# Segment means in two whole operations, and the layer norm of the last two w2 tiles moved into the first w3 groups

## The chip, the cores and the metric

The kernel runs on one core of a Trainium2 chip. The metric is the device time of one execution in microseconds (us). A core has five engines that run at the same time, each with its own queue of instructions: TensorE (PE in the profile, with its weight loads as PEld), VectorE (DVE), ScalarE (ACT), GpSimd (POOL) and SyncE (SP), which issues most of the DMA transfers. They wait for each other by semaphores. Work that lies beside a busy TensorE costs nothing; what makes TensorE wait is added to the time.

## The reference

Two blocks follow each other on x of 2048 tokens by 1024 columns: attention over 64 segments of 32 tokens with an 8-token memory carried from segment to segment, and an MLP with four shifts of the columns. Cut to what matters:

```
h = layernorm(x) * (1 + ca) + sa
x = x + ga * A(h, mem0, Wq, Wk, Wv, Wo)      # 32 heads of 128
h = layernorm(x) * (1 + cb) + sb
x = x + gb * B(h, w1, w2, w3, w4)

def B(x):
    h  = gelu(layernorm(x) @ w1)             # 1024 x 1024
    x1 = x + shifts(h) @ w2                  # 1024 x 1024
    return x1 + gelu(layernorm(x1) @ w3) @ w4   # 1024 x 3584, 3584 x 1024
```

`sa, ca, ga, sb, cb, gb` come from `silu(c) @ w_mod`. Weights and x are bf16.

## The kernel before

Tokens lie in 16 tiles of 128; a transposed operand has the 1024 columns on 128 partitions in 8 pieces (KT = 8). The stages run in this order: the first layer norm, which writes `hh` (h transposed); a first set of projections ("wave 0") for two pairs of heads; a first guess of the segment memories; then attention, in which the projections of later heads and the scores and outputs of earlier heads are woven together; the projection with Wo; the second layer norm; w1; w2; and the stage with w3 and w4. Two orders are at work. Up to w2 a scheduler orders each engine's instructions, within what program order, `keep_order` and added dependencies ask. The stage with w3 and w4 stands under `manual_schedule`, so there the order of the program is the order on each engine.

**Segment means.** The guess of the memories starts from the mean of h over each segment. While the layer norm runs, PE sums the columns of each segment into the PSUM tile `hsum` (L427). `g_prep` (L456) turns the sums into `hbar`, a 128x8x64 tile in bf16: each of the 8 pieces is scaled by its column of `cm` and shifted by its column of `sm_`, the even ones on ScalarE (L462), the odd ones on VectorE (L460); then the first segment, which has another shift, is written over with `m0` in place of `sm_` (L464, L465). `g_v` (L477) multiplies `hbar` with Wv, in eight groups, each with a 1 MB chunk of weights (`wchunk`) and a PSUM tile from a ring of three; `g_o` (L491) does the same with Wo. Between these groups the rest of wave 0 is placed, one projection (L318) at a time. Its PSUM tiles come from the same ring and are emptied by `evac` (L122 on ScalarE, L127 on VectorE).

**Sums of h.** The projections of later heads use a scheme with seven products instead of eight for a 2x2 block, which needs sums and differences of quarters of `hh`: S1, S2, S4 and A21 for each of two halves of the tokens, eight VectorE operations on 128x1920 elements (L519 to L522). In the kernel before they stand behind `ph.close()`, in program order, each held by `keep_order`. The last of the four writes over a quarter of `hh`, so it has to wait until wave 0 has read it. The weights have their own sums (`T_units`, L566 to L569), which wait for the load of the weights. The products are at L623, their joins on VectorE at L595. Scores are at L717, exp at L721, the mask at L723, outputs at L734, and the scaling of the outputs, which frees their PSUM tile, at L741.

**w2 and its layer norm.** `Ba(t)` multiplies tile t with w2 (L1170) into two PSUM tiles; VectorE adds u (`u2`) into `x1b`, a 128x1024 tile in f32, and sums the rows as it goes (L1172). `x1b` is stored in DRAM (L1173). `ln_sums` makes the normalized tile `z` from it: the negative mean `ln_nm` on VectorE (L1147, L1148); the sum of squares on ScalarE (L1150); three operations of one column on GpSimd (`ln_ve` L1152, `ln_rstd` L1154, `ln_nmr` L1156); and the scaling on ScalarE (L1157). `Bb(t)`, one tile later, transposes `z` by DMA into `z2a` (tiles 0 to 7) or `z2b` (tiles 8 to 15). The tiles of this stage, `u2`, `x1b` and `z`, come from the pool `x2_t` with four buffers each. The pools of the next stage lie in part where those of `x2_t` lay, and a first write into such a tile waits for the last reader of what lay there.

**w3.** The stage takes the tokens in two pairs of 512, tiles 0 to 7 and then 8 to 15, each in seven groups over w3 (`w3_stage`) and then w4 (`w4_stage`). A group is again seven products, each for two blocks q of 128 columns and four matmuls long (L1244). They go into the PSUM tiles `bank_b`, `bank_e` and `bank_d`. After the first product into `bank_b`, ScalarE takes a copy (`snap`, L1209), and the third product, which adds to `bank_b`, waits for that copy; between them lies one product into `bank_e`. VectorE joins banks with copies (`join`, L1252) and ScalarE applies gelu (L1248). At the end of a group stand the sums of the next group's weights on VectorE (`w3_sums`, L1098) and one-seventh of the addend units, in which SP loads `x1b` and `x1` back and GpSimd makes the final addend (L1218 to L1223). The sums of `z2a` and the first weights' sums are woven into the last w2 tiles (from tile 10 on). `z2b` is used from the end of pair 0 on.

Of the kernel before, what the change touches and what calls it, by code (L numbers as in the profile page):

```python
# [9 lines left out]
BF16 = mybir.dt.bfloat16  # L10
F32 = mybir.dt.float32
F16 = mybir.dt.float16
I32 = mybir.dt.int32
ACT = mybir.ActivationFunctionType
ALU = mybir.AluOpType
# [4 lines left out]
P = 128  # L20
S = 2048
D = 1024
KT = D // P
# [37 lines left out]
def kernel(ctx, tc, A_x, A_mem0, A_Wq, A_Wk, A_Wv, A_Wo, A_seg_len, B_x, B_w1, B_w2, B_w3, B_w4, c, w_mod, out,  # L61
# [105 lines left out]
    def first_pass(late_hook):  # L167
# [287 lines left out]

        def g_prep():  # L456
            gs["hbar"] = sb1.tile([P, KT, NSEG], BF16, name="hbar")
            for kt in range(KT):
                if kt % 2:
                    nc.vector.tensor_scalar(gs["hbar"][:, kt, :], hsum[:, kt, :], cm[:, kt:kt + 1], sm_[:, kt:kt + 1], ALU.mult, ALU.add)  # L460
                else:
                    nc.scalar.activation(gs["hbar"][:, kt, :], hsum[:, kt, :], ACT.Identity, bias=sm_[:, kt:kt + 1], scale=cm[:, kt:kt + 1])  # L462
            first = sb1.tile([P, KT], F32, name="first")
            nc.vector.tensor_tensor(first[:], hsum[:, :, 0], cm[:], ALU.mult)  # L464
            nc.vector.tensor_tensor(gs["hbar"][:, :, 0], first[:], m0[:], ALU.add)  # L465
            gs["vbarT"] = sb1.tile([P, H, NSEG], BF16, name="vbarT")

        def g_v(g):
# [42 lines left out]
        def f16(ap):  # L511
            return ap.bitcast(F16)

        hA = []
        for p in range(2):
            c0, c1 = slice(2 * p * CH, (2 * p + 1) * CH), slice((2 * p + 1) * CH, (2 * p + 2) * CH)
            A11, A12, A21, A22 = hh[:, 0:4, c0], hh[:, 4:8, c0], hh[:, 0:4, c1], hh[:, 4:8, c1]
            S1, S2, S4 = (hsp.tile([P, 4, CH], F16, name=f"hs{j}{p}")[:] for j in (1, 2, 4))
            keep_order(nc.vector.tensor_tensor(S1, A21, A22, ALU.add))  # L519
            keep_order(nc.vector.tensor_tensor(S2, S1, A11, ALU.subtract))  # L520
            keep_order(nc.vector.tensor_tensor(S4, A12, S2, ALU.subtract))
            keep_order(nc.vector.tensor_tensor(f16(A21), A11, A21, ALU.subtract))  # L522
            hA.append((A11, A12, S4, A22, S1, S2, f16(A21)))
        LA = ExitStack()
        vp = LA.enter_context(tc.tile_pool(name="up_v", bufs=1))
# [604 lines left out]
        def z_sums(pair):  # L1130
# [6 lines left out]
            return [lambda: dve(S1, A21, A22, ALU.add), lambda: dve(S2, S1, A11, ALU.subtract),  # L1137
                    lambda: dve(S3, A11, A21, ALU.subtract), lambda: dve(S4, A12, S2, ALU.subtract)]

        LT2 = ExitStack()  # L1140
        tp = LT2.enter_context(tc.tile_pool(name="x2_t", bufs=4))
        bsm = LT2.enter_context(tc.tile_pool(name="x2_sm", bufs=8))

        def ln_sums(smp, dst, src, sums):

            nm = smp.tile([P, 1], F32, name="ln_nm")
            nc.vector.tensor_tensor(nm[:], sums[:, 0:1], sums[:, 1:2], ALU.add)  # L1147
            nc.vector.tensor_scalar(nm[:], nm[:], -1.0 / D, None, ALU.mult)  # L1148
            sq = smp.tile([P, 1], F32, name="ln_sq")
            nc.scalar.activation(dst, src, ACT.Square, bias=nm[:], accum_out=sq[:])  # L1150
            ve = smp.tile([P, 1], F32, name="ln_ve")
            nc.gpsimd.tensor_scalar(ve[:], sq[:], 1.0 / D, EPS, ALU.mult, ALU.add)  # L1152
            rstd = smp.tile([P, 1], F32, name="ln_rstd")
            nc.gpsimd.tensor_tensor(rstd[:], ve[:], mhalf[:], ALU.pow)  # L1154
            nmr = smp.tile([P, 1], F32, name="ln_nmr")
            nc.gpsimd.tensor_tensor(nmr[:], nm[:], rstd[:], ALU.mult)  # L1156
            nc.scalar.activation(dst, src, ACT.Identity, bias=nmr[:], scale=rstd[:])  # L1157

        def Ba(t):
            def f():  # L1160
                ts = slice(t * P, (t + 1) * P)
                u = tp.tile([P, D], BF16, name="u2")
                nc.sync.dma_start(u[:], u_d[ts, :])
                x1b = tp.tile([P, D], F32, name="x1b")
                sums = bsm.tile([P, 2], F32, name="ln_sums")
                for n2 in range(2):
                    acc = acc_tile()
                    for kt in range(KT):
                        o = 2 + t * P + SHIFT[kt]
                        nc.tensor.matmul(acc[:], lhsT=h1T[:, kt, o:o + P], rhs=w2s[:, kt, n2 * 512:(n2 + 1) * 512], start=(kt == 0), stop=(kt == KT - 1))  # L1170
                    cs = slice(n2 * 512, (n2 + 1) * 512)
                    nc.vector.scalar_tensor_tensor(x1b[:, cs], acc[:], 1.0, u[:, cs], ALU.mult, ALU.add, accum_out=sums[:, n2:n2 + 1])  # L1172
                nc.scalar.dma_start(x1b_d[ts, :], x1b[:])  # L1173
                z = tp.tile([P, D], BF16, name="z")
                ln_sums(bsm, z[:], x1b[:], sums)
                zs[t] = z
            return f

        def Bb(t):
            return lambda: nc.sync.dma_start_transpose(z2s[t // 8][:, :, t % 8 * P:(t % 8 + 1) * P], zs[t][:])  # L1180

        for i, u in enumerate(lagged(Ba, Bb, list(range(NTT)), lag=1)):
            u()
            if i in (4, 8):
                load_upto(ring_ctr[0])
            if i == 10:
                zu = z_sums(0) + w3_sums(0)
            if i >= 10:
                for f in zu[2 * (i - 10):2 * (i - 9)]:
                    keep_order(f())  # L1190
# [36 lines left out]
        def w3_stage(pair):  # L1227

            hq = [[hq_p.tile([P, 14, 512], BF16, name=f"hq{a}{f}") for f in range(2)] for a in range(2)]
            A11, A12, S4, A22, S1, S2, S3 = zsum[pair]
            add = addend_units(pair)
            for g in range(7):
                n = pair * 11 + g
                load_upto(n + 2)
                B11, B21, B22, T4, T1, T2, T3 = ready[n]
                st = [{} for _ in range(2)]

                def prod(bank, A, B, start):  # L1240
                    for q in range(2):
                        acc = st[q][bank]
                        for k in range(4):
                            nc.tensor.matmul(acc[:], lhsT=B[:, k, q * P:(q + 1) * P], rhs=A[:, k, :], start=(start and k == 0), stop=(k == 3), skip_group_check=True)  # L1244
                        yield q

                def gelu(a, f, q, src):
                    nc.scalar.activation(hq[a][f][:, g * 2 + q, :], src[:], ACT.Gelu_apprx_tanh)  # L1248

                def join(a, f, q, bank, s):  # L1250
                    t = stm.tile([P, 512], F32, name="join")
                    nc.vector.tensor_tensor(t[:], st[q][bank][:], st[q][s][:], ALU.add)  # L1252
                    gelu(a, f, q, t)

                for q in range(2):
                    st[q]["b"] = psb.tile([P, 512], F32, name="bank_b")
                for q in prod("b", A11, B11, True):
                    st[q]["s1"] = snap(stA, st[q]["b"])
                for q in range(2):
                    st[q]["e"] = pse.tile([P, 512], F32, name="bank_e")  # L1260
                for q in prod("e", A12, B21, True):
                    join(0, 0, q, "e", "s1")
                dve(T4, B21, T2, ALU.subtract)
                for q in prod("b", S2, T2, False):
                    st[q]["s2"] = snap(st2, st[q]["b"])
                for q in range(2):
                    st[q]["d"] = psd.tile([P, 512], F32, name="bank_d")
                for q in prod("d", S1, T1, True):
                    st[q]["s5"] = snap(stA, st[q]["d"])
                for q in prod("b", S3, T3, False):  # L1270
                    join(1, 1, q, "b", "s5")
                for q in prod("d", S4, B22, False):
                    join(0, 1, q, "d", "s2")
                for q in prod("b", A22, T4, False):
                    gelu(1, 0, q, st[q]["b"])
                for u in w3_sums(n + 1) if g < 6 else []:
                    u()
                for u in add[16 * g // 7:16 * (g + 1) // 7]:
                    u()
            return hq  # L1280
# [97 lines left out]
        with tc.manual_schedule():  # L1378
            for pair in range(2):
                hq = w3_stage(pair)  # L1380
                if pair == 0:
                    LZA.close()
                    rsp = LZ2.enter_context(tc.tile_pool(name="x3_rs", bufs=8))
                    outp = LZ2.enter_context(tc.tile_pool(name="x3_o", bufs=4))
                w4_stage(pair, hq, rsp, outp, late_hook if pair == 1 else None)
# [700 lines left out]
```

## Time and profile before

Three runs took 1485.69, 1487.77 and 1492.43 us; the median is 1487.77. The profiled execution:

| engine | busy us | share of the span | instructions |
|---|---|---|---|
| PE | 1423.4 | 96% | 9198 |
| PEld | 754.6 | 51% | 9254 |
| DVE | 895.3 | 60% | 1946 |
| ACT | 685.7 | 46% | 1443 |
| POOL | 371.8 | 25% | 526 |

The busy share of PE in 40 slices of 37 us is 9 tenths or more in all but the first slice and two others. The places of the change on the profile's clock: the segment means at 63 to 73 us, the sums of h at 112 to 123 us, the border between w2 and w3 at 1128 to 1150 us. A row of the timeline gives start, duration, engine, line and work (output, input, shapes); in brackets stands how long the engine had been idle and who released it. Releasers are inferred from the semaphores, and where an engine waited for several, the last one is named.

### The profile page before, as it was taken

What the parts mean: (1) busy time and instruction counts of PE and PEld (TensorE: products, weight loads), DVE (VectorE), ACT (ScalarE), POOL (GpSimd) and SP (SyncE); (2) the same over time, 40 slices, a digit from 0 to 9 for tenths busy, and PEclk for the clock granted to TensorE, in tenths of its full rate; (3) what the DMA queues carried; (4) which work ended last, traced back from release to release, by engine and by line L of the source; (5) the groups of instructions that cost most, each with busy time, mean ns of one, the idle gap of its engine ahead of it and who ended that gap; (6) DMA issues with size and microseconds to landing.
All of it is one profiled execution on the core that took longest, in us unless ns stands there. A gap on an engine that the chain in (4) does not pass through costs nothing. (4 is left out here: it accounts for less than half of the span.)

```text
span 1488.6 us, 24703 instructions
## 1 busy us (share of the span) xinstructions
PE 1423.4 (96%) x9198; PEld 754.6 (51%) x9254; DVE 895.3 (60%) x1946; ACT 685.7 (46%) x1443; POOL 371.8 (25%) x526
## 2 busy tenths in 40 slices
PE   5898999999999999999998999999998999999998
PEld 3465555565555555555554444444443444444443
DVE  5318777777676777667653244354245668776684
ACT  2715666665665665655552021123465661046400
POOL 7402100000000000000001223213023665646525
PEclk9999999999999999999999999999999999999999
DMA  9677968867777877778579999994398774477812
GB/s 306 204 284 150 192 156 186 193 152 168 167 171 178 191 155 181 156 169 179 109 172 303 352 312 363 327 236 149 97 310 232 230 252 160 135 236 248 278 39 78
DMA packets 404149, 303.48 MB, mean 204 GB/s; under 512 B 199082, under 2 KB 356778, under 8 KB 402226
## 3 DMA queue, kind: packets, MB, share of 16 engines
q1 hardware_dynamic: 365904, 242.06, 61.5%
q10 hardware_dynamic: 29330, 30.89, 6.8%
q0 software_dynamic: 8784, 28.85, 6.6%
q8 instruction: 74, 1.21, 0.4%
q14 instruction: 57, 0.47, 0.1%
HBM read 200.56 MB, written 50.63 MB: 169 GB/s over the span
## 5 line engine op out<-in xcount | busy, mean ns | idle before, releaser
L905 PE MATMUL acc<-wstream,OTc 128*128 128x512 bf16 x940 | 207.8, 379 | 7.7 <-DMA OTc<-OTx_d 3.3
L623 PEld LDWEIGHTS <-T 128*128 128x128 f16 x1408 | 131.4, 98 | 120.4 <-issue 4.4
L591 ACT COPY snap<-acc 128x480 f32<-128x480 f32 x264 | 146.1, 564 | 91.5 <-PE acc L623 83.5
L623 PE MATMUL acc<-hh,T 128*128 128x480 bf16 (+1 forms) x704 | 163.9, 367 | 0.0
L623 PE MATMUL acc<-hs,T 128*128 128x480 f16 x704 | 159.6, 369 | 0.7 <-ACT snap L591 0.6
L905 PEld LDWEIGHTS <-OTc 128*128 128x128 bf16 x960 | 93.3, 98 | 118.8 <-issue 3.9
L759 POOL DMA_DIRECT2D OTx_d<-OT x32 | 24.8, 775 | 439.2 <-DMA OT<-O 372.9
L1244 PEld LDWEIGHTS <-ring 128*128 128x128 f16 (+1 forms) x784 | 77.7, 99 | 106.6 <-issue 16.5
L721 ACT ACTIVATE E<-ps_s 99x495 bf16<-99x495 f32 (+2 forms) x160 | 87.3, 546 | 45.8 <-PE ps_s L717 45.2
L623 PE MATMUL acc<-hh,wq 128*128 128x480 bf16 x464 | 103.9, 366 | 0.0
L741 DVE TENSOR_TENSOR O<-ps_o,rin_all 99x384 bf16<-99x384 f32 (+1 forms) x192 | 97.1, 509 | 3.7
L1098 DVE TENSOR_TENSOR ring<-ring 128x1024 f16<-128x1024 bf16 (+1 forms) x64 | 86.5, 1370 | 5.6 <-PE bank_b L1295 5.2
L734 PE MATMUL ps_o<-V,E 99*128 99x129 bf16 (+1 forms) x704 | 79.6, 220 | 10.6 <-DMA V<-VT 4.8
L595 DVE TENSOR_TENSOR KT<-acc,snap 128x480 bf16<-128x480 f32 x116 | 74.9, 654 | 22.3 <-PE acc L623 19.9
L1295 PEld LDWEIGHTS <-hq 128*128 128x128 bf16 (+1 forms) x560 | 54.7, 98 | 66.1
L1209 ACT COPY snap<-bank_b 128x512 f32<-128x512 f32 x72 | 40.5, 582 | 100.1 <-PE bank_b L1295 58.3
L734 PEld LDWEIGHTS <-E 99*128 99x128 bf16 (+1 forms) x704 | 56.3, 98 | 48.5 <-issue 8.0
L1013 ACT ACTIVATE u<-x,ln_nmr,ln_rstd 128x1024 bf16<-128x1024 f32 x16 | 19.7, 1232 | 127.4 <-DVE ln_nmr L1012 101.6
L723 DVE TENSOR_TENSOR E<-E,maskB 99x495 bf16<-99x495 bf16 (+1 forms) x128 | 48.0, 376 | 49.3 <-ACT E L721 47.4
L1295 PE MATMUL bank_b<-ring,hq 128*128 128x512 f16 (+1 forms) x334 | 73.1, 379 | 0.1
L595 DVE TENSOR_TENSOR VT<-acc,snap 128x480 bf16<-128x480 f32 x90 | 58.0, 650 | 24.9 <-PE acc L623 20.9
L1248 ACT ACTIVATE hq<-join 128x512 bf16<-128x512 f32 x84 | 52.8, 630 | 41.7 <-DVE join L1252 41.7
(243 smaller groups left out, 2527.8 us busy)
## 6 DMA issues: line engine op xcount, KB each, us to landing
wstream<-in_A_Wo_dram SPq DMA_DIRECT2D x31, 1024.0 KB, 11.5
OTx_d<-OT POOLq DMA_DIRECT2D x32, 512.0 KB, 7.0
wstream<-in_B_w_dram SPq DMA_DIRECT2D x28, 512.0 KB, 5.7
OTc<-OTx_d SPq DMA_DIRECT2D x14, 1024.0 KB, 9.5
ring<-in_B_w_dram SPq DMA_DIRECT2D x28, 512.0 KB, 6.3
ring<-in_B_w_dram SPq DMA_DIRECT2D x8, 1792.0 KB, 11.1
wq<-in_A_Wq_dram SPq DMA_DIRECT2D x16, 512.0 KB, 5.1
wk<-in_A_Wk_dram SPq DMA_DIRECT2D x16, 512.0 KB, 7.4
```

The lines of the kernel that those rows point to most:

```text
L591: nc.scalar.copy(t[:], st[q][bank][:, 0:CH])
L595: nc.vector.tensor_tensor(view(d, i), chunks(st[q][bank]), chunks(st[q][s_]), ALU.add)
L623: nc.tensor.matmul(acc[:, 0:CH], lhsT=B[:, k, :], rhs=A[:, k, :], start=(j in (1, 2, 5) and k == 0), stop=(k == 3), skip_group_check=True)
L721: nc.scalar.activation(E[:rows, 0:o], ps[:rows, 0:o], ACT.Exp, scale=DH ** -0.5)
L723: nc.vector.tensor_tensor(E[:rows, 0:o], E[:rows, 0:o], mk[:rows, 0:o], ALU.mult)
L734: nc.tensor.matmul(ps[:, i, :], lhsT=state["e", h, t // 5][:k, c:c + P], rhs=V[:k, t, 0:DH + 1], start=True, stop=True)
L741: nc.vector.tensor_tensor(O[:rows, ts[0]:ts[0] + n, :], ps[:rows, 0:n, 0:DH], rin[:, :, None].to_broadcast([rows, n, DH]), ALU.mult)
L905: mm = nc.tensor.matmul(accs[tt][:], lhsT=ot[hl // 4][:, hl % 4, tt * P:(tt + 1) * P], rhs=woc[hl // 4][:, hl % 4, :], start=(h == 0), sto ...
L1098: return nc.vector.tensor_tensor(dst, a, b, op)
L1244: nc.tensor.matmul(acc[:], lhsT=B[:, k, q * P:(q + 1) * P], rhs=A[:, k, :], start=(start and k == 0), stop=(k == 3), skip_group_check=True)
L1248: nc.scalar.activation(hq[a][f][:, g * 2 + q, :], src[:], ACT.Gelu_apprx_tanh)
L1295: nc.tensor.matmul(acc[:], lhsT=L3[:, k, i * P:(i + 1) * P], rhs=R3[:, k, :], start=(start and k == 0), stop=(k == 13), skip_group_check=True)
```

## The change

The first part makes `hbar` with three operations on VectorE. The whole `hsum` is multiplied by `cm`, the whole result gets `sm_` added, both spread over the 64 segments; then the first segment is written with `m0`. ScalarE has no part in it. The eight sums of h lose their `keep_order`. Instead the first sum of each half waits for the last `hbar` operation, so that the scheduler can put the sums next in line on VectorE once `hbar` is done.

The second part takes tiles 14 and 15 out of the layer norm at the end of w2. Their `x1b`, `z` and small tiles come from new pools (`x2_l`, `x2_lm`, two buffers each) that stay open until pair 0 of w3 is done. Their `ln_sums` and their transposes are put in a list, `late`, and group 0 of w3 runs those of tile 14, group 1 those of tile 15, behind `w3_sums` and ahead of the addend units. What it is for: the border no longer holds the layer norm of the last two tiles between the last w2 product and the first w3 copies.

```diff
         def g_prep():
             gs["hbar"] = sb1.tile([P, KT, NSEG], BF16, name="hbar")
-            for kt in range(KT):
-                if kt % 2:
-                    nc.vector.tensor_scalar(gs["hbar"][:, kt, :], hsum[:, kt, :], cm[:, kt:kt + 1], sm_[:, kt:kt + 1], ALU.mult, ALU.add)
-                else:
-                    nc.scalar.activation(gs["hbar"][:, kt, :], hsum[:, kt, :], ACT.Identity, bias=sm_[:, kt:kt + 1], scale=cm[:, kt:kt + 1])
-            first = sb1.tile([P, KT], F32, name="first")
-            nc.vector.tensor_tensor(first[:], hsum[:, :, 0], cm[:], ALU.mult)
-            nc.vector.tensor_tensor(gs["hbar"][:, :, 0], first[:], m0[:], ALU.add)
+            hs = sb1.tile([P, KT, NSEG], F32, name="hs")
+            nc.vector.tensor_tensor(hs[:], hsum[:], cm[:, :, None].to_broadcast([P, KT, NSEG]), ALU.mult)
+            nc.vector.tensor_tensor(gs["hbar"][:], hs[:], sm_[:, :, None].to_broadcast([P, KT, NSEG]), ALU.add)
+            gs["done"] = nc.vector.tensor_tensor(gs["hbar"][:, :, 0], hs[:, :, 0], m0[:], ALU.add)
...
-            keep_order(nc.vector.tensor_tensor(S1, A21, A22, ALU.add))
-            keep_order(nc.vector.tensor_tensor(S2, S1, A11, ALU.subtract))
-            keep_order(nc.vector.tensor_tensor(S4, A12, S2, ALU.subtract))
-            keep_order(nc.vector.tensor_tensor(f16(A21), A11, A21, ALU.subtract))
+            s1 = nc.vector.tensor_tensor(S1, A21, A22, ALU.add)
+            tc.add_manual_dep(s1.ins, gs["done"].ins.name, mybir.DependencyInfo(mybir.DependencyClass.Sync, mybir.DependencyReason.DATA), reason="segment means first")
+            nc.vector.tensor_tensor(S2, S1, A11, ALU.subtract)
+            nc.vector.tensor_tensor(S4, A12, S2, ALU.subtract)
+            nc.vector.tensor_tensor(f16(A21), A11, A21, ALU.subtract)
...
+        LT3 = ExitStack()
+        tl = LT3.enter_context(tc.tile_pool(name="x2_l", bufs=2))
+        tls = LT3.enter_context(tc.tile_pool(name="x2_lm", bufs=2))
+        late = []
...
-                x1b = tp.tile([P, D], F32, name="x1b")
-                sums = bsm.tile([P, 2], F32, name="ln_sums")
+                pool, small = (tl, tls) if t >= NTT - 2 else (tp, bsm)
+                x1b = pool.tile([P, D], F32, name="x1b")
+                sums = small.tile([P, 2], F32, name="ln_sums")
...
-                z = tp.tile([P, D], BF16, name="z")
-                ln_sums(bsm, z[:], x1b[:], sums)
-                zs[t] = z
+                zs[t] = z = pool.tile([P, D], BF16, name="z")
+                if t >= NTT - 2:
+                    late.extend((lambda: ln_sums(small, z[:], x1b[:], sums), Bb(t)))
+                else:
+                    ln_sums(small, z[:], x1b[:], sums)
...
-        for i, u in enumerate(lagged(Ba, Bb, list(range(NTT)), lag=1)):
+        for i, u in enumerate(lagged(Ba, lambda t: Bb(t) if t < NTT - 2 else lambda: None, list(range(NTT)), lag=1)):
...
-                for u in w3_sums(n + 1) if g < 6 else []:
+                for u in (w3_sums(n + 1) if g < 6 else []) + [late.pop(0) for _ in range(min(2, len(late)))]:
...
                 if pair == 0:
+                    LT3.close()
                     LZA.close()
```

## The prediction

> **What bounds the kernel now.** I read the page first: TensorE (PE) is busy for 96% of the span, so a change pays only where PE stands still or runs slowly. Then PE's waits over the whole run, longest first: who kept it idle, total us, times, longest.
>
> ```profile
> engine line waited for: us in total, times, longest us
> ...
> PE bank_b L1244 <- ACT snap L1209: 7.8, 4, 3.4
> ...
> PE acc L477 <- DVE hbar L465: 4.6, 1, 4.6
> ...
> PE ps_o L734 <- DVE O L741: 4.0, 1, 4.0
> ...
> PE bank_b L1244 <- POOL ln_ve L1152: 1.9, 1, 1.9
> ```
>
> The change touches all four: L465 ends the segment means, L741 follows the sums of h, the other two stand at the border from w2 to w3. Now the timeline at each (start, duration, engine, line, work; in brackets the idle time before and its releaser).
>
> ```profile
> 68.75 0.65 ACT L122 CAST VT<-acc 128x480 bf16<-128x480 f32 x1
> ...
> 70.09 0.54 ACT L462 ACTIVATE hbar<-small_ps,sm,cm 128x64 bf16<-128x64 f32 x1
> 70.66 0.34 DVE L460 TENSOR_SCALAR hbar<-small_ps,cm,sm 128x64 bf16<-128x64 f32 x1 [6.24 <-ACT hbar L462]
> ...
> 72.74 0.20 DVE L465 TENSOR_TENSOR hbar<-first,m 128x8 bf16<-128x8 f32 x1
> ...
> 129.22 0.43 DVE L566 TENSOR_TENSOR T<-wk,wq 128x512 f16<-128x512 bf16 x1 [4.12 <-DMA wk<-in_A_Wk_dram]
> ```
>
> The eight hbar operations alternate between ACT and DVE. ACT's second one stands behind 14 activations of hh and three casts (63.95 to 70.1), and DVE stands 6.24 us behind it. PE is out of work from 68.5 to 73.09. At 129.22 DVE stands behind a load; L741, which PE wants, is queued behind it.
>
> ```profile
> 1130.46 1.24 ACT L1157 ACTIVATE z<-x1b,ln_nmr,ln_rstd 128x1024 bf16<-128x1024 f32 x1 [1.22 <-POOL ln_nmr L1156]
> 1131.60 1.13 ACT L1150 ACTIVATE z<-x1b,ln_nm 128x1024 bf16<-128x1024 f32 x1
> 1134.04 1.24 ACT L1157 ACTIVATE z<-x1b,ln_nmr,ln_rstd 128x1024 bf16<-128x1024 f32 x1 [1.22 <-POOL ln_nmr L1156]
> ...
> 1136.32 0.56 ACT L1209 COPY snap<-bank_b 128x512 f32<-128x512 f32 x1
> 1137.63 1.24 ACT L1157 ACTIVATE z<-x1b,ln_nmr,ln_rstd 128x1024 bf16<-128x1024 f32 x1 [0.75 <-POOL ln_nmr L1156]
> 1138.78 0.57 ACT L1209 COPY snap<-bank_b 128x512 f32<-128x512 f32 x1
> ...
> 1142.22 1.29 DVE L1252 TENSOR_TENSOR join<-bank_e,snap 128x512 f32<-128x512 f32 x2 [12.02 <-DMA z2b<-z]
> ```
>
> The lines at 1130.46, 1134.04 and 1137.63 end the LN of tiles 13, 14 and 15. Both snaps of w3 group 0 stand among them; PE finished bank_e at 1133.57 and waits 3.36 us for the first snap and 1.0 us for the second. A table by stretches shows what that does to the clock (columns: PE, PEld, DVE, ACT, POOL busy, then PEclk).
>
> ```profile
> 1133.60:1136.90 3.30, 0.00 (x0) 0.00 (x0) 0.00 (x0) 2.84 (x4) 0.65 (x4) 1.00 1.07 362
> 1136.90:1144.50 7.60, 6.57 (x16) 2.17 (x16) 1.89 (x3) 3.27 (x5) 0.62 (x2) 0.55 0.82 171
> 1144.50:1149.90 5.40, 5.15 (x25) 2.37 (x25) 3.62 (x5) 4.33 (x9) 4.00 (x4) 1.00 0.95 271
> 1149.90:1162.00 12.10, 12.05 (x57) 5.50 (x57) 9.62 (x11) 8.04 (x15) 7.21 (x8) 1.00 0.83 238
> ```
>
> After the wait 16 matmuls run at about half clock, then full speed returns. Group 0 ends at 1149.88; from there a group takes 12.1 us with PE full.
>
> **What the Trainium skill says.** "TensorE: Matmul & The Clock Gate", Part 1, says that PE drops to half rate after an idle window of about 3.4 us and recovers after a busy one. This trace agrees in the main: mean clock 0.58, 0.55 and 0.55 after waits of 4.6, 4.0 and 3.4 us, none after the wait of 1.95 us. The same page (Architectural detail) says that ScalarE and VectorE queues are strictly in order; the snap at 1138.78, whose bank was full 7 us earlier, agrees. "SBUF — State Buffer", section "SBUF: two separate sides", says that a VectorE operation with two SBUF inputs and a GpSimd operation lock each other out of a shared port. Agrees: the three w3 sums (L1098) take 4.26 us beside GpSimd's addends (1148.96), 2.01 us without (1173.13).
>
> **The change part by part.**
>
> *Segment means.* It removes 4 ACT operations (1 x 0.40 ahead of the hh activations, the rest behind them), and 6 on DVE. It adds three on DVE. No row has a broadcast operand; the nearest, 128x512 from PSUM with an SBUF operand (L1252), takes 0.69 us. I take 2 x 0.69 + 0.20 (as L465) = 1.6 us; bounds 1.2 and 3.0 change nothing, for DVE is free from 63.9, so hbar is ready by 67 and PE asks at 68.5. A new limit takes over: the first L477 matmul needs the PSUM tile that ACT's VT cast frees, now 0.3 to 0.7 us earlier, at about 68.75. Gain 73.09 - 68.75 = 4.3 us. The first 64 matmuls then took 3.26 us at half clock; later 32 take 1.10, so 64 take 2.2: 1.0 more. **-5.3** (-4.3 to -5.7).
>
> *Sums of h.* The eight sums (1.15 us each, 112.7 to 123.1) go behind hbar. Seven run between 65.5 and 75, where DVE has only copies of 0.42 us to do, so they cost nothing: a vbarT copy may come 1 us late, but three PSUM tiles rotate and the next is wanted 3 us later. The last (L522 for the second half) still waits until about 105, when its columns have been read. DVE then leaves 123 clear, and the first O results pass ahead of the blocked T sums. The load at 129.2 (PE's clock) does not move in relation to PE, though, so from 131.0 DVE has the listed rest: four VT joins 2.5, two O 1.1, two masks 0.64, three reciprocals 0.5 = 4.8 us, to 135.8. Before, it reached this place at 137.72. PE itself could gain 3.4 us, but DVE is nearly full until 150 (9.49 of 10 us), so I count DVE's lead: **-1.9** (-1.0 to -3.5).
>
> *LN of tiles 14 and 15, at the border.* With their ln_nm pairs gone, the last L1172 ends 0.6 us sooner; PE starts w3 at 1129.35 and has finished bank_e at 1132.8. The first snap no longer stands behind LN 14. But in the built program it now waits for the transpose of z of tile 13, because the snap tiles have come to lie over x2_t. That transpose is issued at 1131.73, as before. The one before it took 4.23 us to land, uncontended ones 3.2, this one 7.8 beside two ring loads that now queue behind it. I take 4.2: snap at 1136.0, PE at 1136.7. The wait has changed its cause and hardly its end. The second snap and the joins follow at once, however; so 40 matmuls x 0.216 = 8.64, plus 1.7 for one half-clock window, end group 0 at 1147.05 instead of 1149.88: **-2.8** (-1.0 with the transpose at 6 us, -4.6 without a slow window).
>
> *LN inside groups 0 and 1.* This adds a wait on ACT, in front of the next group's snaps. Counting from the group's last matmul: the w3 sums on DVE, ahead of ln_nm in its queue, end at +1.1 if POOL is idle; ln_nm at +1.5; L1150 with its accumulator read 1.31; the three POOL steps 1.13; L1157 1.15 until ACT is free; snap 0.6: +5.75. PE wants that snap after two products, at +3.46. **+2.3** for tile 14 (1.6 if ln_nm hides behind the gelu). For tile 15 POOL is not idle: two addend units (3.4 us each) lie ahead of ln_ve in its queue, and their loads stand behind the transpose of tile 14 on SP, so they fall on this very border. They slow the sums (to +3.5) and hold ln_ve until about +5.5. Then 1.1 + 1.15 + 0.6: snap at +8, **+4.5** (1.6 to 6.5). A gap of that length drops the clock once, likely: **+1.2**. Later transposes and ring loads have a whole group of slack: nothing.
>
> Sum: -5.3 - 1.9 - 2.8 + 2.3 + 4.5 + 1.2 = -2.0, so 1487.8 - 2.0 = **1485.8 us**. Between these places PE is full, so shifts are carried to the end.
>
> **The rivals.** (a) The LN is hidden: POOL's addends miss the border and group 0 starts at full clock. Then -4.6 + 1.6 + 1.6 = -1.4 for the border, with -8.6 ahead of it (both upper ends nearly): -10, 1477.8. For it: ACT is busy for only 8.04 of 12.1 us a group, and LN adds 2.6. Against it: ACT waits in order while POOL works. (b) Slower: the transpose takes 6 us (-1), the stalls are 2.3 and 6.5, two slow windows 3.4, and DVE's lead is lost (-3.2 in all ahead): +8, 1495.8. For it: the 7.8 us landing and the crowding of POOL. (c) The hbar wait turns into one for a Wv or Wo chunk, as ten 1 MB loads have 2.5 us each: -2 ahead, +5.2 at the border: 1491. Against it: no such wait today, and later loads keep their distance to PE.
>
> **How the numbers follow.** Forecast 0.5, (a) 0.25, (b) 0.13, (c) 0.12. The range leaves out (b) and reaches past (a): 1477 to 1493.5. Faster by 0.5% is below 1480.3: (a) and a little of the forecast, 0.26; slower is above 1495.2: (b), 0.13; the rest 0.61.
>
> **What would show it.** PE's wait for hbar gone or under 1 us, with full clock at the first L477; S sums in 65 to 75; L741 ahead of the blocked L566. At the border the first snap released by a z2b transpose; then new PE waits for a snap at the start of groups 1 and 2, with L1157 just ahead of it. No such waits, or a wait for wchunk, would prove me wrong.

## The result and the profile after

The changed kernel takes **1497.2 us** (median of 4 runs, 1495.6 to 1500.5), the kernel before 1487.5 beside it: a ratio of 1.0063, 95% interval 1.0034 to 1.0092. It is slower; 1485.8 was forecast, with a range that ended at 1493.5.

First PE's waits over the whole run of the changed kernel (who kept it idle: us in total, times, longest). (On the page of the kernel before, PE is below nine tenths in six of the 40 slices, not in three.) L477 and L734 of before are L473 and L731 here, L1209 and L1244 are L1213 and L1248, L1295 is L1299.

```profile
PE bank_b L1248 <- ACT snap L1213: 15.6, 4, 6.2
...
PE bank_e L1299 <- DVE hq L1095: 4.2, 1, 4.2
PE bank_e L1299 <- DVE join L1321: 4.2, 1, 4.2
...
PE bank_b L1248 <- DMA z2b<-z: 1.7, 1, 1.7
...
PE acc L473 <- ACT VT L122: 1.0, 1, 1.0
```

The wait for hbar (4.6) is gone, with 1.0 left for the cast behind it, and of the wait for O (4.0) 0.2 is left. The wait ahead of the first w3 matmul, 1.9 before, is 1.7 and now put down to a transpose. The wait for snaps, 7.8 before, has doubled; the forecast named the new ones. But two waits of 4.2 us are new **in w4**, a stage that the change doesn't touch and that had no wait before.

A table of two stretches shows what that is worth: w3 of pair 0, then w4 of pair 0. The kernel before comes first, the changed one second (start and end, length, PE, PEld, DVE, ACT, POOL busy, PEclk, DMA share, GB/s).

```profile
1129.96:1222.40 92.44, 87.51 (x386) 38.97 (x394) 52.58 (x69) 61.10 (x104) 49.42 (x52) 0.96 0.80 242
1222.40:1307.00 84.60, 84.39 (x389) 38.34 (x392) 64.55 (x40) 7.83 (x14) 48.12 (x29) 1.00 0.45 150
```

```profile
1119.43:1221.73 102.30, 89.91 (x392) 39.46 (x393) 51.37 (x71) 61.46 (x104) 44.69 (x48) 0.93 0.70 206
1221.73:1319.03 97.30, 88.90 (x393) 39.24 (x392) 64.34 (x40) 7.75 (x14) 54.56 (x33) 0.95 0.47 152
```

w3 begins 10.5 us earlier (1129.96 - 1119.43); w3 then takes 9.9 longer and w4 12.7 longer; the rest, pair 1 and the tail, gives back 2.0. Sum: +10.1, the difference of the two spans (1498.7 - 1488.6).

These are two single executions, though, each some 3 us longer than its kernel's median (1490.4 and 1500.5 us). In e2 below, where nothing ahead of the border is changed, w3 also begins 4.8 us earlier than in this profile of before, so the lead that the change made is nearer 6 us than 10.5. The larger part of the loss is w4's.

Now the places that the forecast named. The segment means, on DVE's and ACT's timeline:

```profile
61.98 0.68 DVE L459 TENSOR_TENSOR hs<-small_ps,cm 128x512 f32<-128x512 f32 x1
62.69 0.69 DVE L460 TENSOR_TENSOR hbar<-hs,sm 128x512 bf16<-128x512 f32 x1
63.42 0.19 DVE L461 TENSOR_TENSOR hbar<-hs,m 128x8 bf16<-128x8 f32 x1
63.74 1.16 DVE L515 TENSOR_TENSOR hs<-hh 128x1920 f16<-128x1920 bf16 x1
...
66.97 0.64 ACT L122 CAST VT<-acc 128x480 bf16<-128x480 f32 x1
```

Both whole operations take what the nearest row took (0.69), hbar is there at 63.6, and the sums of h follow at once. The first L473 matmul starts at 67.66, released by the VT cast. Now ACT at the border and at the start of groups 1 and 2:

```profile
1128.62 1.08 ACT L1213 COPY snap<-bank_b 128x512 f32<-128x512 f32 x2 [6.89 <-DMA z2b<-z]
...
1143.80 1.24 ACT L1158 ACTIVATE z<-x1b,ln_nmr,ln_rstd 128x1024 bf16<-128x1024 f32 x1 [1.22 <-POOL ln_nmr L1157]
1144.94 1.05 ACT L1213 COPY snap<-bank_b 128x512 f32<-128x512 f32 x2
...
1160.24 1.24 ACT L1158 ACTIVATE z<-x1b,ln_nmr,ln_rstd 128x1024 bf16<-128x1024 f32 x1 [1.23 <-POOL ln_nmr L1157]
1161.39 1.05 ACT L1213 COPY snap<-bank_b 128x512 f32<-128x512 f32 x2
```

The first snap is released by a transpose into z2b, the next two stand directly behind a late LN's Identity, as forecast.

Lastly w4. It has seven products too, of 56 matmuls each (12.1 us). DVE opens it with two sums over hq (the output of w3) of 7168 elements a partition. Then come T1, the difference of two loaded chunks of weights (B12 - B11), which the third product needs; the first joins and results o; and two more hq sums, which the fourth product needs. A result o adds the addend, loaded back from DRAM as rs. The load of B12 is called the w4 load from here on. First DVE at T1 (L1095), then SyncE's queue in front of the w4 load (L1109), in the changed kernel:

```profile
1245.70 3.89 DVE L1095 TENSOR_TENSOR ring<-ring 128x7168 f16<-128x7168 bf16 x1 [14.37 <-DMA ring<-in_B_w_dram]
```

```profile
1232.49 0.32 SPq L1222 DMA_DIRECT2D xb<-x1b_d  x1
1236.05 0.32 SPq L1224 DMA_DIRECT2D x<-x_d  x1
1236.48 1.52 SPq L1109 DMA_DIRECT2D ring<-in_B_w_dram  x2
```

The w4 load is issued 14.8 us into w4, directly behind the last addend load. Before, it went out 1.6 us into w4, behind the same load:

```profile
1223.59 0.32 SPq L1220 DMA_DIRECT2D x<-x_d  x1
1224.04 1.44 SPq L1112 DMA_DIRECT2D ring<-in_B_w_dram  x2
```

In the changed kernel it takes some 9 us to land (1236.48 to 1245.70), so T1 is late, DVE's joins behind T1 are late, and PE waits until 1250.25. At 1263.4, one product on, it waits again, for the hq sums queued behind those joins and results.

### The profile page after: what moved, and what is told of

Same layout as the page of the kernel before. It is cut to its first block, busy times and chain, and to the rows that moved or that the text cites. A ratio compares the mean times of both kernels' runs of the same rounds, so it can differ in the third digit from the quotient of the medians.

```text
span 1498.7 us, 24747 instructions
## 1 busy us (share of the span) xinstructions
PE 1429.1 (95%) x9254; PEld 753.9 (50%) x9254; DVE 895.8 (60%) x1943; ACT 684.0 (46%) x1439; POOL 371.3 (25%) x526
## 4 chain that ended last, share of the span: by engine, by line
PE 70%; DMA 10%; DVE 7%; POOL 5%; issue 4%; ACT 4%; ACTq 0%; SPq 0%; POOLq 0%; DVEq 0%
PE acc L620 30%; PE acc L902 7%; PE bank_b L1299 6%; PE bank_b L1248 4%; PE acc L1069 4%; PE acc L328 3%; PE acc L318 3%; PE acc L1172 2%; PE ps_o L731 2%; PE bank_d L1248 2%; DMA xb<-x1b_d 2%; PE bank_e L1299 2%; PE ps_s L714 2%; PE bank_d L1299 2%; DMA V<-VT 1%
## 5 line engine op out<-in xcount | busy, mean ns | idle before, releaser
L588 ACT COPY snap<-acc 128x480 f32<-128x480 f32 x264 | 146.3, 565 | 87.5 <-PE acc L620 80.2
L1248 PEld LDWEIGHTS <-ring 128*128 128x128 f16 (+1 forms) x784 | 77.7, 99 | 114.4 <-issue 24.5
L738 DVE TENSOR_TENSOR O<-ps_o,rin_all 99x384 bf16<-99x384 f32 (+1 forms) x192 | 97.0, 509 | 3.7
L1095 DVE TENSOR_TENSOR ring<-ring 128x1024 f16<-128x1024 bf16 (+1 forms) x64 | 87.7, 1389 | 17.5 <-DMA ring<-in_B_w_dram 14.4
L1299 PEld LDWEIGHTS <-hq 128*128 128x128 bf16 (+1 forms) x560 | 55.3, 99 | 72.6 <-DVE hq L1095 4.7
L1213 ACT COPY snap<-bank_b 128x512 f32<-128x512 f32 x72 | 40.4, 583 | 109.6 <-PE bank_b L1299 60.1
L731 PE MATMUL ps_o<-V,E 99*128 99x129 bf16 (+1 forms) x704 | 79.5, 220 | 8.4 <-DMA V<-VT 5.7
L731 PEld LDWEIGHTS <-E 99*128 99x128 bf16 (+1 forms) x704 | 56.2, 98 | 46.0 <-issue 6.0
L1299 PE MATMUL bank_b<-ring,hq 128*128 128x512 f16 (+1 forms) x336 | 73.2, 379 | 0.0
L1248 PE MATMUL bank_b<-zs,ring 128*128 128x512 f16 x224 | 56.3, 397 | 15.6 <-ACT snap L1213 15.6
```

The costliest lines, as they stand in the source:

```text
L588: nc.scalar.copy(t[:], st[q][bank][:, 0:CH])
L731: nc.tensor.matmul(ps[:, i, :], lhsT=state["e", h, t // 5][:k, c:c + P], rhs=V[:k, t, 0:DH + 1], start=True, stop=True)
L738: nc.vector.tensor_tensor(O[:rows, ts[0]:ts[0] + n, :], ps[:rows, 0:n, 0:DH], rin[:, :, None].to_broadcast([rows, n, DH]), ALU.mult)
L1095: return nc.vector.tensor_tensor(dst, a, b, op)
L1299: nc.tensor.matmul(acc[:], lhsT=L3[:, k, i * P:(i + 1) * P], rhs=R3[:, k, :], start=(start and k == 0), stop=(k == 13), skip_group_check=True)
```

## The experiments

**The theory at first** was that a late transpose on SyncE's in-order queue holds up the addend loads behind it, and these the w4 load. Rivals: GpSimd's in-order queue, the tiles' new places in memory, or the earlier arrival of w3. The table sets the twelve runs side by side: the ratio to runs of the kernel before taken beside them (medians from 1486.1 to 1488.1) with its 95% interval, the lengths of w3 and w4 of pair 0 in the profiled run, and where the **add of the 14th of 16 addend units** starts on GpSimd, counted from the start of w4 (in brackets how long it takes). With two buffers the loads of the 16th and last unit wait for the 14th, so this add tells when SyncE's queue comes free.

| kernel | median us | ratio | w3 | w4 | 14th add |
|---|---|---|---|---|---|
| before | 1487.5 | 1 | 92.4 | 84.6 | -3.6 (1.27) |
| after | 1497.2 | 1.0063 [1.0034, 1.0092] | 102.3 | 97.3 | +5.9 (4.80) |
| e1 means and sums of h | 1479.7 | 0.9957 [0.9943, 0.9971] | 92.4 | 84.9 | -2.4 (1.27) |
| e2 late LN alone | 1502.6 | 1.0119 [1.0102, 1.0137] | 99.6 | 97.2 | +6.1 (4.79) |
| e3 transposes behind addend loads | 1491.5 | 1.0035 [1.0018, 1.0053] | 95.3 | 96.2 | +5.9 (4.80) |
| e4 w4 load first | 1493.6 | 1.0053 [1.0036, 1.0070] | 97.4 | 95.6 | +11.1 (1.27) |
| e5 addends ahead of LN | 1492.2 | 1.0048 [1.0029, 1.0067] | 104.0 | 85.2 | -1.3 (1.27) |
| e6 e1, addends a group later | 1484.2 | 0.9988 [0.9977, 0.9998] | 96.8 | 84.6 | -2.0 (1.27) |
| e7 LN split | 1487.4 | 1.0006 [0.9990, 1.0023] | 90.1 | 94.8 | +5.9 (4.79) |
| e8 LN split, z apart | 1482.8 | 0.9972 [0.9962, 0.9981] | 84.7 | 96.0 | +5.9 (4.80) |
| e9 after, third x13 buffer | 1484.1 | 0.9972 [0.9961, 0.9982] | 97.1 | 85.3 | +0.4 (1.27) |
| e10 e1, third x13 buffer | 1478.2 | 0.9934 [0.9918, 0.9950] | 96.8 | 84.6 | -11.4 (1.50) |
| e11 e8, third x13 buffer | 1471.9 | 0.9902 [0.9874, 0.9931] | 84.8 | 84.6 | -0.7 (1.28) |
| e12 means alone | 1482.5 | 0.9968 [0.9955, 0.9980] | 92.4 | 84.6 | -2.3 (1.28) |

w4 knows two lengths. Where the 14th add starts at most 0.4 us into w4, it is 84.6 to 85.3 us; where it starts 5.9 us or more into it, 94.8 to 97.3. In the first group the w4 load goes out at most 4.0 us into w4, in the second 14.7 to 14.9 us into it (e4 moves it ahead). The length of w3 is less firm: with the border of before it was 92.4 us in three kernels (before, e1, e12) and 96.8 in two (e6, e10), so 4 us there in a single profile tell little.

**e1 and e2: the parts apart.** e1 takes the edits of g_prep and of the sums of h alone, e2 the rest alone.

> Only the segment means and the sums of h are changed; the border from w2 to w3 is that of before. Theory (the two parts ahead of attention pay as forecast, the loss is all behind w2): L477's wait for hbar and the wait for O both gone, the attention stages run 7 to 9 us earlier, 1487.5 - 8 = 1479.5 us. Rival (what is won ahead is given back at the loads of Wo and OTc, which do not move with PE): the lead is down to 2 or 3 us by the end of the Wo stage, 1485 us.

> Only the LN of the last two tiles is moved; segment means and sums of h are those of before. Theory (the loss is this part's own, and adds up with the other): w3 of pair 0 takes 102 us instead of 92.4, w4 of pair 0 97 instead of 84.6, so 1487.5 + 9.9 + 12.7 = 1510 us, 1505 if the lead of the other parts was 8 and not 10.5. Rival (the waits in w4 come from the earlier arrival of w3 against its loads, so they need both parts): w4 as before, 1497 us.

e1 gained 6.4 us (0.0043 x 1486), its w3 and w4 are those of before. e2 lost 17.7, with both waits of w4. The parts add up (-6.4 + 17.7 = +11.3 against +9.4 in the comparison of after), within the intervals, so the waits in w4 are no effect of an earlier arrival; and late LN costs about 18 us by itself.

**e3: SyncE's order alone.**

(Code in this part is cut to what matters.)

```
-for u in w3_sums(n+1) + late[:2]: u()           # LN, then its transpose
-for u in add[...]: u()
+for u in w3_sums(n+1) + late[:1] + add[...] + late[1:2]: u()
```

> The changed kernel with one order changed: on the SyncE queue the transpose of a late tile is issued behind the addend loads of its group, not ahead of them; ACT, DVE, GpSimd keep their order. Theory (a transpose that waits for its LN holds up the addend loads behind it, those hold up the addends on GpSimd, and these the addend loads ahead of the w4 loads seven groups later): both 4.4 us waits in w4 and their two half-clock windows go, -12; the addends of group 0 also leave GpSimd before LN 15, so the stall of group 2 falls from 4.4 to 2.1 us without a slow window, -5: 1480 us; 1485 if only the first half holds. Rival (GpSimd, which now does LN 14 and 15 ahead of its addends, is what is late, or the tiles' new places in memory): the order on SyncE changes little, w4 keeps its waits, 1492 to 1497 us.

Half right. The stall of group 2 fell to 2.0 us and w3 to 95.3. But w4 stayed at 96.2: the theory in its first form falls. GpSimd did the first addend unit 22.4 us into w3 (before: 15.5), behind LN 14's three steps, and the third 36.5 (before: 24.1), behind those of LN 15.

**e4: the w4 load out of the queue.** load_upto(n + 2) became load_upto(n + 2 + (g == 6)).

> The changed kernel with one load moved, in both pairs: the w4 chunk whose sum DVE waited 14.4 us for (B12) is issued ahead of the addend loads of group 6 instead of behind them. The waits at the border and in groups 1 and 2 stay. Theory (the load stood in the SyncE queue behind late addend loads): the first wait in w4 and its half-clock window go, -6; the second (hq sums behind results that wait for loads of rs) shrinks by 2 to 6: 1485 to 1489 us. Rival (the load was late because of bandwidth or of its ring slot, not of its place in the queue): the wait stays above 3 us, 1495 to 1498 us.

Another miss, and a useful one. The first wait went, the second grew to 7.9 us, and w4 was hardly shorter. What DVE waited for in w4 of this kernel:

```profile
DVE o L1325 <- POOL rs L1319: 8.4, 2, 7.9
```

The results o need addends read back from rs, and those come last of all: GpSimd itself waited 4.3 us for that load. The load was only the first that the late addends held up; with it out of the way the next one binds.

**e5: addends ahead of late LN on both queues.** The order became w3_sums, the group's addends, then LN and transpose.

> The changed kernel with one order changed: the late LN of a group (DVE, ACT, GpSimd and its transpose on SyncE) is issued behind the group's addend units, so on both in-order queues (SyncE and GpSimd) the addends stand where they stood before. e3 moved them on SyncE alone, and w4 of pair 0 still took 96.2 us. Theory (on GpSimd the third addend unit stood behind LN 15, 11 us later than without late LN, and the chain of addends, 5.7 us a unit, never catches up): w4 of pair 0 is back at 85 to 86 us; LN 15 now waits for addends instead, so w3 takes 97 to 98.5: 1479.7 + 5.5 + 0.5 = 1486 us. Rival (w4's waits come from the late LN in another way: tiles' places in memory, or ACT and DVE): w4 stays at 96 to 97 us, 1494 to 1497 us.

w4 was back at 85.2 as expected, yet w3 took 104.0 (97 to 98.5 expected) and the total was 6 us above the figure given. The theory gets no credit for w4. Counted from the start of w3, the 14th unit's store came at 104.3 us, in e3 at 106.3, so the order bought 2 us of the chain; the rest is that w3 itself was 8.7 us longer and so ended later. This pointed to the pair of numbers in the table: what counts is the chain's end against w3's end.

**e6: a late chain without late LN.** In e1, add[16g/7 : 16(g+1)/7] became add[16(g-1)/6 : 16g/6], none in group 0.

> No LN is moved at all: the kernel of e1 (segment means and sums of h alone), in which the 16 addend units of a pair are issued in groups 1 to 6 instead of 0 to 6, in both pairs. Theory (a late start of the addend chain alone makes the waits in w4, since 16 units of 5.7 us fill the 92 us of w3 and the last loads stand ahead of the w4 load): w3 of pair 0 stays at 92.4 us, w4 of pair 0 rises from 84.9 to 95 or more, and w4 of pair 1 too: 1479.7 + 10 to 22 = 1490 to 1502 us. Rival (the chain has slack and catches up, the late LN itself is at fault): 1480 us.

The figure missed (1490 or more expected, 1484.2 measured), and the trace says that the test was weak: SyncE runs ahead of PE, so the first unit moved only from 15.3 to 17.9 us, while w3 was 4.4 us longer in this profile (the first joins waited for a transpose). The chain was still in time. It tells no more than that so small a delay is borne.

**e7 and e8: late LN without its waits.** Taken apart in groups 0 and 2, and in e8 with z in a pool of its own:

```
+lt = late.pop(0) if late and g in (0, 2) else [nothing] * 4
...
 st[q]["s5"] = snap(stA, st[q]["d"])
+lt[1]()                              # Square, and GpSimd's three steps
...
 gelu(1, 0, q, st[q]["b"])
+lt[2]()                              # Identity
+for u in w3_sums(n+1) + add[...] + [lt[3]]: u()
```

> The changed kernel with late LN taken apart: the Square goes behind the bank_d snaps of groups 0 (tile 14) and 2 (tile 15), where ACT waits for joins, GpSimd's three steps directly behind it, the Identity behind the group's last gelu, the transpose behind the group's addend loads. The snap tiles still lie over the tiles of w2, so the first snap still waits for tile 13's transpose. Theory: the stalls of groups 1 and 2 go, w3 takes 84.6 + 3.4 for the transpose + 1.8 of half clock = 90 us, addends start a little late at most, w4 85 to 88: 1476 to 1480 us. Rival (ACT is too full for LN within a group, snaps come late anyway): w3 above 94 us, 1484 us or more.

> e7, and z of all w2 tiles in a pool of its own (three buffers, closed after w3 of pair 0), so the snap tiles lie over u2 and x1b alone and the first snap no longer waits for a transpose of z. Theory (the memory under the snap tiles made the first wait of the border): PE's wait at group 0 goes with its half-clock window, w3 takes 85 us, w4 85: 1479.7 - 7.4 = 1472 us, faster than both kernels. Rival (the first snap is late for another reason, a store of x1b or LN 13 on ACT): a wait of 2 to 3.5 us stays, 1476 to 1478 us.

For w3 both figures held: 90.1 and 84.7 us, the latter without a wait from its first matmul on (1.3 us are left ahead of it, 1.9 before). So the place in memory (snap tiles over z) made the border's wait, and the place of late LN in the queues the stalls of groups 1 and 2. But w4 rose to 94.8 and 96.0, so both totals missed, by 7 us or more and by 11. e8, with the border repaired, is no faster than e1, which keeps the border of before (0.9972 against 0.9957, the intervals overlap). Their w3 and w4:

```profile
1120.30:1212.69 92.39, 86.77 (x392) 38.71 (x393) 52.64 (x69) 61.09 (x104) 48.10 (x51) 0.98 0.79 240
1212.69:1297.56 84.87, 84.78 (x394) 38.26 (x393) 65.98 (x40) 7.83 (x14) 52.26 (x30) 1.00 0.47 153
```

```profile
1116.31:1201.01 84.70, 84.70 (x392) 38.31 (x393) 56.73 (x71) 60.55 (x106) 47.09 (x48) 1.00 0.85 244
1201.01:1296.99 95.98, 89.16 (x394) 39.29 (x393) 66.20 (x40) 7.73 (x14) 55.08 (x33) 0.95 0.46 152
```

In e1 (first pair of lines) w3 and w4 take 177.3 us together, in e8 180.7. The 8 us at the border, which the change set out to win, could not be won with this chain of addends: it needs the 92 us that w3 had. Counted from the start of w3, the 14th multiply comes even earlier in e8 than in e1 (87.5 us against 88.6); only w3 ends sooner. **The theory in its second form**: the chain (load, two operations on GpSimd, store, two buffers) takes 73.3 us from the first unit's multiply to the 14th's in e1, 5.6 us a unit, and 76.6 in e8; it ends with w3, and if it ends later, w4 waits.

**e9, e10 and e11: a faster chain.** x13, the tile that a unit adds into and stores from, gets three buffers instead of two: in the changed kernel, in e1, and in e8 (there one join buffer pays for it).

```
+rs3 = tc.tile_pool(name="x3_r3", bufs=3, side="right")
-x1 = rsq.tile([P, 512], F32, name="x13")
+x1 = rs3.tile([P, 512], F32, name="x13")
```

> The changed kernel with three buffers instead of two for x13, the tile that an addend unit on GpSimd adds into and stores from; nothing else. In the runs so far a unit's load of x13 is issued 3 to 6 us after the store of the unit two before it, and a unit takes about 5.7 us. Theory (w4 waits because the addend chain, paced by its buffers, ends too late for the w4 load behind it): with a load bound to the store three units back a unit takes about 4.2 us, the chain makes up its late start within w3 (46 + 14 x 4.2 = 105 us behind the start of w3, which takes 97 to 102), the w4 load comes near the start of w4, and w4 of pair 0 takes 85 to 88 us: 1497 - 11 = 1486 us. Rival (the chain is paced by bandwidth or by the order on SyncE, not by buffers): w4 stays at 95 us or more, 1495 us.

> The kernel of e1 (segment means and sums of h alone, LN of before) with three buffers for x13. Control for e9. Theory (the buffers matter only where the chain is late): the chain ends earlier and nothing waits for it, w4 stays at 84.6 to 84.9, 1479.7 us. Rival (a third buffer helps w3 or w4 in general, for instance by fewer addends beside DVE's sums): 2 us or more faster, 1477 us or less.

> e8 (late LN split, z apart: w3 of pair 0 took 84.7 us without a wait, w4 96.0) with three buffers for x13, paid for with one of the four join buffers. Theory: the chain is done when the shorter w3 ends, both waits in w4 and their half-clock windows go, -11: 1472 us, faster than both kernels and than e1. Rival (e8's waits in w4 come from the load itself, now asked for 8 us earlier than the queues can bring it): w4 stays above 92 us, 1481 us or more. The fourth join buffer is not expected to matter; if it does, joins show waits for gelu.

e9: 1484.1 (1486 expected), w4 85.3; the whole loss in w4 is gone, with late LN where the change put it. The w4 load goes out 2.6 us into w4, not 14.8. The reason given holds only in part, though. From the first multiply to the 14th the chain took 69.9 us in e9 against 74.1 in the changed kernel, 5.4 instead of 5.7 us a unit and not the 4.2 expected. In e11 it is 71.7 against 76.6 in e8. So the 14th multiply comes 3.7 us earlier against the start of w4, from 2.7 us behind it to 1.0 us ahead (from e8 to e11 4.8 us, from 2.8 behind to 2.0 ahead). The third buffer does a second thing, which the expectation left out: the last x13 load no longer waits for the store of the 14th unit to land. In the changed kernel that load stood 3.6 us behind the xb load ahead of it (1232.49 and 1236.05 above), in e9 0.4:

```profile
1217.08 0.32 SPq L1223 DMA_DIRECT2D xb<-x1b_d  x1
1217.49 0.38 SPq L1225 DMA_DIRECT2D x<-x_d  x1
1218.01 1.90 SPq L1109 DMA_DIRECT2D ring<-in_B_w_dram  x2
```

Together these few us are worth 11 to 12 in w4.

e10: in w4 nothing changed, as expected. Its interval overlaps e1's, but its ratio is 3 us lower (0.9934 against 0.9957), so a small gain of the third buffer by itself is not excluded; the 13 us from the changed kernel to e9 are far more.

e11: 1471.9 (1472 expected), w3 and w4 both without a stall from the first w3 matmul on (1.8 us ahead of it) and at full clock:

```profile
1119.79:1204.60 84.81, 84.81 (x392) 38.35 (x393) 57.47 (x71) 60.44 (x106) 49.12 (x50) 1.00 0.91 261
1204.60:1289.22 84.62, 84.62 (x393) 38.29 (x392) 66.50 (x40) 7.91 (x14) 58.17 (x32) 1.00 0.48 155
```

It beats the kernel before by 14.6 us (0.0098 x 1488.1), the changed kernel by more, and e1. Against e10, which has the third buffer and the border of before, it is 4.8 us ahead (0.9902 against 0.9934), but these two intervals overlap (0.9918 to 0.9931), so what the moved LN is worth once the chain is fast is shown by the traces alone (w3 in 84.8 us).

**Why w4 has two lengths.** The 14th unit on GpSimd, in the kernel before and then in the changed one:

```profile
1217.39 1.26 POOL L1221 TENSOR_TENSOR xb<-xb,gb_b 128x512 f32<-128x512 f32 x1 [4.35 <-DMA xb<-x1b_d]
1218.78 1.27 POOL L1222 TENSOR_TENSOR x<-xb,x 128x512 f32<-128x512 f32 x1
```

```profile
1224.43 3.15 POOL L1225 TENSOR_TENSOR xb<-xb,gb_b 128x512 f32<-128x512 f32 x1 [2.88 <-DMA xb<-x1b_d]
1227.66 4.80 POOL L1226 TENSOR_TENSOR x<-xb,x 128x512 f32<-128x512 f32 x1
```

What DVE did meanwhile in the changed kernel, the two hq sums that open w4:

```profile
1222.57 3.89 DVE L1095 TENSOR_TENSOR zs<-hq,hq 128x7168 f16<-128x7168 bf16 x1 [1.67 <-ACT hq L1252]
1226.49 4.84 DVE L1095 TENSOR_TENSOR hq<-hq,hq 128x7168 f16<-128x7168 bf16 x1
```

The multiply and the add take 3.15 and 4.80 us instead of 1.26 and 1.27, and end 1.1 us behind the ends of DVE's two sums (1227.58 and 1226.46, 1232.46 and 1231.33). The Trainium skill ("SBUF — State Buffer", section "SBUF: two separate sides") calls this a lock and not a sharing of bandwidth, and these lines agree: GpSimd gets on when DVE's operation is over.

A 14th unit that meets the sums therefore ends 11 us into w4, whatever the run (its store is issued at +11.0 in after, e3, e7 and e8, at +11.2 in e2). With two buffers the last x13 load waits for that store to land, and the w4 load waits behind it. A unit done just ahead of the sums leaves the queue free at +1.5 to +4. Before, the 15th unit met the same two sums (3.97 and 4.79 us), but no load in front of the w4 load waits for it. In e4 the 14th unit came later still and behind the sums (add at +11.1, 1.27 us). That reading fits all runs; no run takes DVE's sums away to test the lock by itself.

**e12: segment means alone.**

> Segment means in two whole operations alone; the sums of h and the border are those of before. Theory (the prediction's terms: 4.3 for the wait and 1.0 for the clock): PE's wait at the first L477 is 0 to 1 us, the wait for O at the start of attention stays, 1486.5 - 5.3 = 1481.2 us, 1 to 2 us slower than e1. Rival (sums of h pay nothing by themselves, all of e1's gain is the means): the same as e1, 1479.7 us.

4.8 us (0.0032 x 1488), 5.3 forecast. PE's wait for O is still there:

```profile
PE ps_o L730 <- DVE O L737: 3.9, 1, 3.9
```

In e1 0.2 us of that wait is left, and its stretch from the first score to the first Wo matmul is 663.0 us against 664.8 here: 1.8 for the sums of h (1.9 forecast). The intervals of the two times overlap, so the traces carry this part. Over all kept traces the stretch takes 661.5 to 664.2 us in the eleven kernels with the new sums (median 662.3) and 664.4 to 666.7 in the three without (before, e2, e12; median 664.8), so the gain is there, at some 2 us.

## Why the prediction was wrong

The forecast was -2.0 us, the measured difference +9.7 (1497.2 - 1487.5). Point by point, by the forecast's own steps:

- **Segment means: right.** -5.3 forecast, -4.8 measured alone (e12). PE's wait in front of the first L473 matmul fell from 4.6 to 1.0 us, and the limit that took over is the VT cast, as said. The half-clock stretch went.
- **Sums of h: right.** Seven of the eight run from 63.7 to 72.1 beside the copies, L738 passes ahead of the blocked T sums, and about 2 us came of it (-1.9).
- **The border: the mechanism right, the size a spread.** -2.8 rested on a transpose that lands in 4.2 us. In the changed kernel's profile tile 13's was issued at 1121.76 and the snap it releases began at 1128.6, some 6.8 us, and PE waited 6.2; in e2, e3 and e4 PE's wait there was 3.0 to 3.5 us, less than the forecast's 3.9 (1132.8 to 1136.7). The 6 us that the forecast allowed for the transpose covered it nearly.
- **LN in groups 1 and 2: right.** Stalls of 2.3 and 4.5 us were forecast; PE's waits in the trace are 2.0 and 4.2. The clock was put at 1.2; in the trace PE ran 5.6 us at half clock behind the second stall (1162.0 to 1167.6), which costs 2.8. All of w3: 92.4 + 5.2 = 97.6 forecast; 102.3 in the profile of after (the slowest of its four runs), 97.4 and 99.6 in e4 and e2.
- **The step that failed**: "Later transposes and ring loads have a whole group of slack: nothing." It priced the late LN at 0 beyond the border and the two groups. In w4 it cost **12.7 us**, and with that the sum changed its sign. The prediction saw each piece: the addend loads behind the transpose on SP, the addends and LN 15 in one GpSimd queue. It asked what they do to LN's end, not what LN does to theirs. Before, the chain's 14th add ended 2.3 us ahead of w4 (-3.6 + 1.27), and the busy shares don't show that: GpSimd is busy for 49 of 92 us and looks free. In the changed kernel it started 5.9 us behind w4's start. e9, which gives the chain a third buffer and leaves all else, takes the 12 us back.

Rival (b), 1495.8, came nearest in time, but not by its reason: it had DVE's lead lost and longer stalls at the border, and the lead was kept. What none of the cases had is that the 8 us lost at the border also gave the addends time. e8 shows it: with the border repaired w4 takes 11 us more than in e1. Taking w4's 12.7 us off the measured 1497.2 gives 1484.5, an estimate that lies inside the range; e9, which has no such loss, took 1484.1.

## What to carry to other kernels

Before moving work onto in-order queues, follow each queue to its last instruction in the stage and ask who waits for that one: slack is measured at the end of a chain of loads, operations and stores, not where the work is put in. A wait on the busiest engine may be what lets a slower chain finish; look for the chain that ends with the stage before pricing the wait as gain. A chain with two buffers may then be helped more by a third than by a new order (here the third buffer took the ratio from 1.0063 to 0.9972, 13 us; the two changes of order, e3 and e5, to 1.0035 and 1.0048).

## What was not expected of the hardware

- A small delay on GpSimd can grow to a fixed one: an add of 1.27 us took 4.80 us where it met DVE's 4.84 us sum. Together with the multiply ahead of it, this put the 14th unit's store 11.0 us into w4 in four runs, though w3 lasted from 84.7 to 102.3 us in them.
- The time from issue to landing of a transpose into z2b lay between 3.0 and 8.2 us within the 50 us around the border of the changed kernel, and PE's wait that hangs on it was 3.0 to 6.2 us in runs with the same border. A forecast that hangs on one landing needs that width.
- The length of a wait did not settle whether the clock fell. In e9 PE waited 3.5 us at the border and went on at full clock, and waited 2.1 us at the start of group 1 and soon went on at half clock. Both waits are counted from 0.2 us after the start of the last matmul ahead, the spacing of matmuls here. Columns as in the tables above; the first stretch follows the longer wait:

```profile
1125.20:1128.60 3.40, 3.35 (x16) 1.56 (x16) 1.89 (x3) 3.13 (x6) 0.00 (x0) 1.00 0.92 251
...
1140.40:1143.80 3.40, 3.40 (x10) 1.18 (x9) 0.94 (x2) 2.06 (x4) 0.00 (x0) 0.50 0.89 176
```

16 matmuls run in the one stretch, 10 in the other. The Trainium skill ("TensorE: Matmul & The Clock Gate", Part 1, "What's actually happening") says that the clock is set by free-running windows of 3.4 us, and the trace agrees: the half-clock stretches of this run begin at 1140.40 and 1157.5, five windows of 3.41 us apart, and last 3.41 us each. Counted back on that grid, the longer wait (1121.8 to 1125.25) falls into two windows and fills 45% and 56% of them; the shorter one (1137.33 to 1139.47) lies in one window and fills 63%. The same count over all fourteen traces, from 1090 to 1335 us: of the windows at full clock in which PE was idle for a quarter or more, all 39 with an idle share of 65% or more were followed by half clock, none of the 39 with up to 62%, and of five at 63% three. So a window need not be idle throughout, though the page's "idle window" reads that way and the forecast took it so.

The forecast's 1.7 us beside a long wait depends on the place of the wait on the grid, which a change of a few us ahead of it moves.
